# Attention and two MLPs on one core: the second MLP's first operands loaded during the last slots of the first MLP

## The chip, the core and the metric

The kernel runs on one core of one Trainium2 chip. The metric is the time of one execution on the device in microseconds (us), lower is better. Three runs of the kernel before took 1113.15, 1113.36 and 1116.99 us; their median is 1113.36 us.

## What is computed

A chunked attention, then two MLPs of 3072 tokens, one after the other, each 512 to 2048 to 512 wide:

```python
attn_out = _attn_ref(**attn_kwargs)             # 4 x 8 x 768 x 64, chunks of 32 with 8 memory keys
x = attn_out.transpose(0, 2, 1, 3).reshape(B * S, H * D)
h = x @ w_in                                    # first MLP
x = np.where(h > 0.0, h, np.exp(np.minimum(h, 0.0)) - 1.0) @ w_out
r = np.maximum(x @ w_in2, 0.0)                  # second MLP
out = (s * (r * r) + b) @ w_out2
```

Every large product is made of three products of halves: an operand is split into a rounded part (hi) and the rest (lo), and hi·hi, hi·lo and lo·hi are added up (`mm3`, lines 323 to 325).

## The kernel before

**First MLP.** The tokens are cut into eight tiles of 384. For each tile there are 16 slots, one for each 128 of the 2048 hidden columns. Slot `c` of tile `t` is `h1(t, c)`: twelve matmuls into a PSUM bank `psH`, the activation on ScalarE (ACT) and VectorE (DVE) (lines 347 to 349), and the split into `gh` and `gl`. Two slots later `out1(t, c)` adds the slot's part to four accumulators `acc` with twelve more matmuls. After a tile's last slot `put_out` copies the four accumulators into `big` tiles, two on ACT and two on DVE (lines 377 and 379), and SyncE (SP) stores them to `y_dram` (line 380). A `big` tile comes from the pool `op`, two buffers in tiles 5 to 7, or, where `big_tile` is told `spare`, from the pool `wst` of three. Attention runs beside the first tiles.

**Weights.** The first MLP's weights stay in SBUF, split, in the pool `wp`: 32 tiles of 4 KB a partition, two for each slot number (`w0_c` for `h1`, `w1_c` for `out1`). The second MLP's weights are turned into seven block combinations for each 256 hidden columns (`prepare`, tiles 5 to 7, pool `prep`) and stored to `s_dram`. `prepared` spreads 160 such steps over the half slots of tiles 5 to 7.

**Second MLP.** It works on three tiles of 1024 tokens with a seven-product scheme (`ORDER`). `load_blocks(t)` loads four blocks of 512 KB from `y_dram` (line 611), makes three differences on DVE (line 614), and splits seven operands `xc`: seven copies on ACT (line 618) and seven subtractions on DVE (line 181). `next_piece` loads the weight pieces `ws`, 256 KB each, twelve buffers deep (line 596). `first_layer` multiplies, and takes its first two products out of PSUM with `aside` (ACT, line 630) into the pool `evp`, since the third accumulates in the first one's bank.

**What sets the order.** Each engine and SP's queue run their instructions in the order in which a scheduler wrote them down, which follows the order of the program's calls and may move an instruction ahead. Between the MLPs all pools of the first are closed (`pctx.close(); mctx.close()`), then the pools of the second are opened on the same memory, and `for _ in load_blocks(0): pass` comes before the first matmul:

```python
    pctx.close()
    mctx.close()
...
    for _ in load_blocks(0):
        pass
    for t in range(NT2):
```

At the start SP loads `kb` and `q` of unit 0, the two scalars `s_sb` and `b_sb` (lines 461 and 462; 128 elements of 4 bytes each), and then `kb` and `q` of unit 1.

Of the kernel before, what the change touches and what calls it, by code (L numbers as in the profile page):

```python
# [8 lines left out]
F32 = mybir.dt.float32  # L9
I32 = mybir.dt.int32  # L10
# [18 lines left out]
NU0 = 6  # L29
HF = 6  # L30
TATT = 5
MICRO = 8
HN, NT2 = 512, 3
ORDER = (1, 2, 6, 5, 7, 3, 4)
# [18 lines left out]
def tile_attention_then_two_mlps(ctx, tc, q_in, k_in, v_in, w1, w2, s_in, b_in, out):  # L53
# [34 lines left out]
    const = ctx.enter_context(tc.tile_pool(name="const", bufs=1))  # L88
    dp = ctx.enter_context(tc.tile_pool(name="dp", bufs=1, space=bass.MemoryType.DRAM))
    mctx = ExitStack()  # L90
    wp = mctx.enter_context(tc.tile_pool(name="wp", bufs=1))
    wst = mctx.enter_context(tc.tile_pool(name="wst", bufs=3))
    one = mctx.enter_context(tc.tile_pool(name="one", bufs=1))
    xp = mctx.enter_context(tc.tile_pool(name="xp", bufs=1))
# [18 lines left out]
    def f(t):  # L113
        return t.bitcast(F32)
# [3 lines left out]

    def load_w(w, c, i):

        r = wp.tile([P, DM, 2], I32, tag=f"w{i}_{c}", name=f"raw{i}_{c}")
        nc.sync.dma_start(out=r, in_=w[c, i].bitcast(I32).rearrange("p (n z) -> p n z", z=2))
        return r

# [14 lines left out]
    def split_w(c, i, raw):  # L139

        t = wst.tile([P, DM], I32, tag="t", name="t")
        yield from to_f32(raw, t)
        nm = "io"[i]
        parts = wp.tile([P, 2, DM], F32R, tag=f"w{i}_{c}", name=f"w{i}_{c}")
        hi, lo = parts[:, 0], parts[:, 1]
        nc.scalar.activation(out=hi, in_=f(t), func=AF.Copy)
        sub(lo, f(t), hi)
        W[nm, c], WT[nm, c] = (hi, lo), parts
        yield
# [30 lines left out]
    def sub(lo, src, hi):  # L180
        return nc.vector.tensor_tensor(out=lo, in0=src, in1=f(hi), op=ALU.subtract)  # L181

    def big_tile(n, spare=False):

        if spare:
            return wst.tile([P, DM], F32, tag="t", name="big")[:, :n]
        return op[-1].tile([P, n], F32, tag="big", name="big")
# [173 lines left out]
    def put_out(t, c, n):  # L361

        split, t0 = t == 0, starts[t] * U
        if c == HF and split:
            for m in range(KT):
                PART[m] = big_tile(n)
                nc.sync.dma_start(out=PART[m], in_=part_dram[:, m, :n])
        if c == NF - 1 or c == HF - 1 and split:
            for m, acc in enumerate(ACC[t]):
                with tc.high_priority(400):  # L370
                    if c == NF - 1 and split:
                        o = PART.pop(m)
                        nc.vector.tensor_tensor(out=o, in0=o, in1=acc[:, :n], op=ALU.add)
                    else:
                        o = big_tile(n, m == 3 and t >= 2)
                        if m % 2:
                            nc.vector.tensor_copy(o, acc[:, :n])
                        else:
                            nc.scalar.activation(out=o, in_=acc[:, :n], func=AF.Copy)  # L379
                nc.sync.dma_start(out=y_dram[:, m, t0:t0 + n] if c == NF - 1 else part_dram[:, m, :n], in_=o)  # L380

    def out1(t, c):
        n = sizes[t] * U
# [43 lines left out]
    def prepare_all():  # L427
        for layer in range(2):
            for i in range(NF // 2):
                yield from prepare(layer, i)  # L430
# [27 lines left out]

    warm(6, pt.rearrange("p h n -> p (h n)")[:, :2 * U])
    set_up()  # L460
    nc.sync.dma_start(out=s_sb, in_=s_in.to_broadcast([P, 1]))
    nc.sync.dma_start(out=b_sb, in_=b_in.to_broadcast([P, 1]))

    nload = [1, 0]

# [27 lines left out]
    def weights_to(w, n, ahead):  # L493

        while wnext[0] < min(n, MICRO * NF):
            k, m = divmod(wnext[0], MICRO // 2)
            c, i = divmod(k, 2)
            load_ws(w, k + 1 + ahead)
            if m == 0:
                wsteps[:] = [split_w(c, i, wraw[k])]  # L500
            next(wsteps[0])
            wnext[0] += 1
# [7 lines left out]
    def beside(want, weights):  # L510
# [6 lines left out]
            weights_to(w, n0 + (n - n0) * (done[0] - d0) // (want - d0), ahead)  # L517
        weights_to(w, n, ahead)

    def mlp1_step(t, c):  # L520

        phase[0] = (1 if c < HF else 3) if t == 0 else 2 if t == 1 else 4

        a0, total, k, ks = done[0], 0, 0, 1
        if t == 0 and c < HF:
            a0, total, k, ks = ready[0], ready[1] - ready[0], c, HF
        elif t == 0:
            a0, total, k, ks = ready[1], ready[2] - ready[1], min(c - HF, NF - HF - 4), NF - HF - 3
        elif 1 < t < TATT:
            a0, total, k, ks = ready[2], len(steps) - ready[2], NF * (t - 2) + c, NF * (TATT - 2)  # L530

        wt = [(w1, 0, 4)] * 2
        if t == 0 and c < HF:
            n0, n1 = 12, 8 * HF + 12
            wt = [(w1, max(n0 + (n1 - n0) * (2 * c + z) // (2 * HF), MICRO * (c + z)), 4) for z in (1, 2)]
        elif t == 1:
            n0 = 8 * HF + 12
            wt = [(w1, max(n0 + (MICRO * NF - n0) * (2 * c + z) // 28, MICRO * (c + z)), 4) for z in (1, 2)]
        if c == 0 and t == TATT:
            actx.close()  # L540
            op.append(mctx.enter_context(tc.tile_pool(name="op2", bufs=2)))
            p2["prep"] = mctx.enter_context(tc.tile_pool(name="prep", bufs=2, reuse_waits="tile"))
            p2["steps"] = prepare_all()
        if t < 2:
            weights_to(w1, MICRO * (c + 1), 4)
        h1(t, c)
        beside(a0 + total * (2 * k + 1) // (2 * ks), wt[0])
        prepared(t, 2 * c + 1)
        yield
        beside(a0 + total * (2 * k + 2) // (2 * ks), wt[1])  # L550
        prepared(t, 2 * c + 2)
        if c == NF - 4 and 1 <= (t or 1) < NTILE1 - 1 and t != 1:
            load_x(max(t, 1) + 1)
        yield

    def prepared(t, n):

        want = NPREP * (2 * NF * (t - TATT) + n) // (2 * NF * (NTILE1 - TATT))
        while t >= TATT and p2["n"] < want:
            next(p2["steps"])  # L560
            p2["n"] += 1
# [11 lines left out]
    for slot in seq[-2:]:  # L573
# [2 lines left out]
    pctx.close()  # L576
    mctx.close()

    xcp, yrp, wsp, g2p, evp, ghp, outp = (
        ctx.enter_context(tc.tile_pool(name=nm, bufs=k, reuse_waits="tile"))  # L580
        for nm, k in (("xcp", 1), ("yrp", 4), ("wsp", 12), ("g2p", 4), ("evp", 5), ("ghp", 3), ("outp", 4)))
    psp = ctx.enter_context(tc.tile_pool(name="psp", bufs=8, space=PSUM, reuse_waits="tile"))

    def bank(nm):
        return psp.tile([P, HN], F32, tag="b", name=nm)

    pieces = [(0, i, j) for i in range(NF // 2) for j in ORDER] + [(1, i, j) for j in ORDER for i in range(NF // 2)]
    pieces = pieces * NT2
    ws, used = [], [0]

    def next_piece(layer, i, j):

        while len(ws) < min(used[0] + 11, len(pieces)):
            lay, ii, jj = pieces[len(ws)]
            w = wsp.tile([P, 2, 2 * P], F32R, tag="ws", name="ws")
            nc.sync.dma_start(out=f(w), in_=s_dram[lay, ii, :, PIECE[jj]])
            ws.append(w)
        assert pieces[used[0]] == (layer, i, j)
        used[0] += 1
        return ws[used[0] - 1]  # L600

    XC = {}

    def load_blocks(t):

        t0 = t * 2 * HN
        xc = XC[t] = {j: xcp.tile([P, 2, 2, HN], F32R, tag=f"xc{j}", name=f"xc{j}") for j in ORDER}
        b12 = yrp.tile([P, 2, HN], F32, tag="yr", name="b12")
        b11, b21, b22 = (f(xc[j][:, 1]) for j in (1, 2, 3))
        for o, r, z in ((b11, 0, 0), (b12, 0, 1), (b22, 1, 1), (b21, 1, 0)):  # L610
            nc.sync.dma_start(out=o, in_=y_dram[:, 2 * r:2 * r + 2, t0 + z * HN:t0 + (z + 1) * HN])
        t3, t2, t4 = (yrp.tile([P, 2, HN], F32, tag="yr", name=nm) for nm in ("t3", "t2", "t4"))
        for o, x, y in ((t3, b22, b12), (b12, b12, b11), (t2, b22, b12), (t4, b21, t2)):
            nc.vector.tensor_tensor(out=o, in0=x, in1=y, op=ALU.subtract)
            yield
        src = {1: b11, 2: b21, 6: t2, 5: b12, 7: t3, 3: b22, 4: t4}
        for j in ORDER:
            nc.scalar.activation(out=xc[j][:, 0], in_=src[j], func=AF.Copy)
            sub(xc[j][:, 1], src[j], xc[j][:, 0])
            yield  # L620

    def add(o, x, y):
        return nc.vector.tensor_tensor(out=o, in0=x, in1=y, op=ALU.add)
# [89 lines left out]
                        nc.scalar.activation(out=r, in_=o[m], func=AF.Copy)  # L713
                    put(r, t, 2 + m, 0)

    for _ in load_blocks(0):
        pass
    for t in range(NT2):
        gs = [g2p.tile([P, 4, 2, HN], F32, tag="g", name="g2") for _ in range(NF // 4)]
        for i in range(NF // 2):  # L720
# [59 lines left out]
```

## Time and profile before

| | |
|---|---|
| median of three runs | 1113.36 us |
| the profiled execution: its own time | 1114.08 us |
| the profiled execution: its span | 1112.3 us |
| mean granted TensorE clock | 0.985 |
| TensorE (PE) busy | 1072.5 us, 96% of the span |
| DVE busy | 785.8 us, 71% |
| ACT busy | 593.3 us, 53% |
| DMA: HBM read and written | 164.89 MB and 47.45 MB, 191 GB/s |

Busy times are shares of the whole span, and a matmul's end is modelled. Where PE waits is read from the slices of the span, and then from the timeline of the place. The execution that was profiled has a time of its own, 1.78 us over its span.

### The profile page before, as it was taken

What the parts mean: (1) busy time and instruction counts of PE and PEld (TensorE: products, weight loads), DVE (VectorE), ACT (ScalarE), POOL (GpSimd) and SP (SyncE); (2) the same over time, 40 slices, a digit from 0 to 9 for tenths busy, and PEclk for the clock granted to TensorE, in tenths of its full rate; (3) what the DMA queues carried; (4) which work ended last, traced back from release to release, by engine and by line L of the source; (5) the groups of instructions that cost most, each with busy time, mean ns of one, the idle gap of its engine ahead of it and who ended that gap; (6) DMA issues with size and microseconds to landing.
All of it is one profiled execution on the core that took longest, in us unless ns stands there. A gap on an engine that the chain in (4) does not pass through costs nothing.

```text
span 1112.3 us, 20640 instructions
## 1 busy us (share of the span) xinstructions
PE 1072.5 (96%) x8206; PEld 965.0 (87%) x8206; DVE 785.8 (71%) x1299; ACT 593.3 (53%) x939; POOL 0.7 (0%) x6
## 2 busy tenths in 40 slices
PE   6989999999999999999999599999999999999998
PEld 4879999999999999999999577778888788888886
DVE  6899856777777777998882267598356697266854
ACT  3888544344344337887773355555255654355442
POOL 0000000000000000000000000000000000000000
PEclk8899999999999999999999889999999999999999
DMA  8955032433434217889770476777866777776674
GB/s 307 372 199 223 1 107 86 150 133 100 140 115 143 88 40 251 332 312 325 286 281 30 162 222 187 229 221 211 252 190 191 226 215 211 225 197 190 190 213 128
DMA packets 98112, 213.70 MB, mean 192 GB/s; under 512 B 9952, under 2 KB 27360, under 8 KB 95968
## 3 DMA queue, kind: packets, MB, share of 16 engines
q1 hardware_dynamic: 98016, 212.38, 58.8%
q8 instruction: 65, 1.06, 0.4%
q14 instruction: 31, 0.25, 0.1%
HBM read 164.89 MB, written 47.45 MB: 191 GB/s over the span
## 4 chain that ended last, share of the span: by engine, by line
PE 75%; DVE 9%; DMA 7%; ACT 5%; issue 2%; SPq 0%; DVEq 0%; ACTq 0%
PE psH L323 13%; PE psH L324 12%; PE psH L325 12%; PE psL L324 6%; PE psL L325 6%; PE psL L323 6%; PE acc L323 5%; PE acc L325 5%; PE acc L324 5%; DMA xc<-y_dram 2%; DMA raw<-w 2%; PE psVS L275 1%; DVE pt L255 1%; DVE t L132 1%; ACT raw L129 1%
## 5 line engine op out<-in xcount | busy, mean ns | idle before, releaser
L323 PE MATMUL acc<-gh,w 128*128 128x384 f32 x512 | 171.6, 337 | 5.1 <-ACT big L379 2.3
L323 PE MATMUL psH<-xh,w 128*128 128x384 f32 x512 | 174.3, 341 | 0.9 <-DVE g L349 0.6
L324 PE MATMUL psH<-xl,w 128*128 128x384 f32 x512 | 172.6, 337 | 0.2 <-DVE xl L181 0.2
L325 PE MATMUL psH<-xh,w 128*128 128x384 f32 x512 | 172.4, 337 | 0.0
L324 PE MATMUL acc<-gl,w 128*128 128x384 f32 x512 | 171.5, 335 | 0.0
L325 PE MATMUL acc<-gh,w 128*128 128x384 f32 x512 | 171.3, 335 | 0.0
L323 PE MATMUL psH<-xc,ws 128*128 128x512 f32 x336 | 133.6, 402 | 13.4 <-DMA ws<-s_dram 11.8
L679 ACT ACTIVATE g2h<-g 128x1024 fp32r<-128x1024 f32 x84 | 88.9, 1059 | 90.1 <-PE psL L325 89.8
L324 PE MATMUL psL<-g2l,ws 128*128 128x512 f32 x336 | 130.9, 390 | 1.9 <-DVE g2l L181 1.9
L324 PE MATMUL psH<-xc,ws 128*128 128x512 f32 x336 | 131.8, 392 | 0.9 <-DVE xc L181 0.9
L325 PE MATMUL psH<-xc,ws 128*128 128x512 f32 x336 | 131.8, 392 | 0.0
L325 PE MATMUL psL<-g2h,ws 128*128 128x512 f32 x336 | 130.7, 389 | 0.0
L181 DVE TENSOR_TENSOR g2l<-g,g2h 128x1024 fp32r<-128x1024 f32 x84 | 102.2, 1223 | 39.5 <-ACT g2h L679 39.2
L323 PE MATMUL psL<-g2h,ws 128*128 128x512 f32 x336 | 130.1, 389 | 0.0
L347 ACT ACTIVATE g<-psH 128x384 f32<-128x384 f32 x128 | 62.6, 489 | 116.6 <-PE psH L325 77.0
L177 ACT ACTIVATE gh<-g 128x384 fp32r<-128x384 f32 x128 | 67.0, 523 | 87.9 <-DVE g L349 87.1
L349 DVE SCALAR_TENSOR_TENSOR g<-g,psH 128x384 f32<-128x384 f32 x128 | 70.6, 551 | 58.9 <-ACT g L348 57.8
L323 PEld LDWEIGHTS acc<-gh,w 128*128 128x128 f32 x512 | 95.9, 188 | 7.5 <-ACT big L379 2.9
L323 PEld LDWEIGHTS psH<-xh,w 128*128 128x128 f32 x512 | 96.9, 189 | 3.2 <-DVE g L349 1.2
L324 PEld LDWEIGHTS psH<-xl,w 128*128 128x128 f32 x512 | 96.9, 189 | 0.4 <-DVE xl L181 0.4
L325 PEld LDWEIGHTS psH<-xh,w 128*128 128x128 f32 x512 | 97.0, 189 | 0.0
L324 PEld LDWEIGHTS acc<-gl,w 128*128 128x128 f32 x512 | 96.1, 188 | 0.4 <-DVE gl L181 0.4
(97 smaller groups left out, 1668.2 us busy)
## 6 DMA issues: line engine op xcount, KB each, us to landing
ws<-s_dram SPq DMA_DIRECT2D x336, 256.0 KB, 3.0
raw<-w SPq DMA_DIRECT2D x64, 512.0 KB, 5.8
s_dram<-right SPq DMA_DIRECT2D x16, 1024.0 KB, 4.8
kb<-k SPq DMA_DIRECT2D x24, 512.0 KB, 5.6
v<-v SPq DMA_DIRECT2D x24, 512.0 KB, 4.7
s_dram<-left SPq DMA_DIRECT2D x16, 768.0 KB, 4.1
q<-q SPq DMA_DIRECT2D x24, 256.0 KB, 5.4
y_dram<-big SPq DMA_DIRECT2D x32, 192.0 KB, 2.0
```

The costliest lines, as they stand in the source:

```text
L129: nc.scalar.activation(out=low, in_=low.bitcast(U32), func=AF.Copy, scale=2.0 ** -29 * (1 - 2.0 ** -15), bias=-0.4999)
L132: nc.vector.scalar_tensor_tensor(out=t, in0=high, scalar=3, in1=low, op0=ALU.logical_shift_left, op1=ALU.bitwise_or)
L177: return nc.scalar.activation(out=hi, in_=src, func=AF.Copy)
L181: return nc.vector.tensor_tensor(out=lo, in0=src, in1=f(hi), op=ALU.subtract)
L255: nc.vector.transpose(out=pt[k * CH:(k + 1) * CH, :, rows], in_=sm[rows, :, z, n0:n0 + CH])
L275: nc.tensor.matmul(ps[r % 2 * D:(r % 2 + 1) * D, z, o:o + CH], v[rows, (r * NC + c) * D:(r * NC + c + 1) * D], pt[rows, r, cs], start=True ...
L323: nc.tensor.matmul(o, sa(a[0]), sb(b[0]), start=first, stop=False, skip_group_check=again)
L324: nc.tensor.matmul(o, sa(a[0]), sb(b[1]), start=False, stop=False, skip_group_check=again)
L325: return nc.tensor.matmul(o, sa(a[1]), sb(b[0]), start=False, stop=last, skip_group_check=again)
L347: nc.scalar.activation(out=g[:, :n], in_=ps[:, :n], func=AF.Relu, scale=-1.0)
L349: nc.vector.scalar_tensor_tensor(out=g[:, :n], in0=g[:, :n], scalar=-1.0, in1=ps[:, :n], op0=ALU.add, op1=ALU.max)
L679: nc.scalar.activation(out=gh, in_=g[:, block], func=AF.Copy)
```

## The change

- The pool `wp` is cut in two: `wpa` with the sixteen weight tiles of slots 0 to 7 (`NFREE = 8`), on the right side of the memory, and `wpb` with the others. `prep` moves to the right side, next to `wpa`.
- In tile 7, before `h1` of slot 10, `prep` and `wpa` are closed and the second MLP's pools `xcp`, `yrp` and `wsp` are opened there. `load_blocks(0)` now also loads the first twelve weight pieces, and is advanced three steps after each of slots 10 to 15.
- `prepared` has to be through with its 160 steps 16 half slots earlier.
- In tiles 5 to 7 three of the four `big` tiles come from `wst`. In tile 7 the stores are issued by ACT in place of SP.
- `s_sb` and `b_sb` are loaded at the start of tile 5, and no more at the start of the kernel.

```diff
-    wp = mctx.enter_context(tc.tile_pool(name="wp", bufs=1))
+    early = [ExitStack(), ExitStack()]
+    wps = [early[0].enter_context(tc.tile_pool(name="wpa", bufs=1, side="right")),
+           mctx.enter_context(tc.tile_pool(name="wpb", bufs=1))]
...
-                        o = big_tile(n, m == 3 and t >= 2)
+                        o = big_tile(n, t >= TATT and m > 0 or m == 3 and t >= 2)
...
-                nc.sync.dma_start(out=y_dram[:, m, t0:t0 + n] if c == NF - 1 else part_dram[:, m, :n], in_=o)
+                store = nc.scalar if t == NTILE1 - 1 else nc.sync
+                store.dma_start(out=y_dram[:, m, t0:t0 + n] if c == NF - 1 else part_dram[:, m, :n], in_=o)
...
     set_up()
-    nc.sync.dma_start(out=s_sb, in_=s_in.to_broadcast([P, 1]))
-    nc.sync.dma_start(out=b_sb, in_=b_in.to_broadcast([P, 1]))
...
+    def load_blocks(t):
...
+        for o, r, z in ((b11, 0, 0), (b12, 0, 1), (b22, 1, 1), (b21, 1, 0)):
+            nc.sync.dma_start(out=o, in_=y_dram[:, 2 * r:2 * r + 2, t0 + z * HN:t0 + (z + 1) * HN])
+        if t == 0:
+            load_pieces(12)
...
+    def open_second():
+
+        for nm, k in (("xcp", 1), ("yrp", 4), ("wsp", 12)):
+            p2[nm] = ctx.enter_context(tc.tile_pool(name=nm, bufs=k, side="right", reuse_waits="tile"))
+        p2["blocks"] = load_blocks(0)
...
+            p2["prep"] = early[1].enter_context(tc.tile_pool(name="prep", bufs=2, side="right", reuse_waits="tile"))
             p2["steps"] = prepare_all()
+            nc.sync.dma_start(out=s_sb, in_=s_in.to_broadcast([P, 1]))
+            nc.sync.dma_start(out=b_sb, in_=b_in.to_broadcast([P, 1]))
...
+        if t == NTILE1 - 1 and c == NFREE + 2:
+            early[1].close()
+            early[0].close()
+            open_second()
         h1(t, c)
...
+        if t == NTILE1 - 1 and c >= NFREE + 2:
+            for _ in range(3):
+                next(p2["blocks"], None)
...
-        want = NPREP * (2 * NF * (t - TATT) + n) // (2 * NF * (NTILE1 - TATT))
+        want = min(NPREP * (2 * NF * (t - TATT) + n) // (2 * NF * (NTILE1 - TATT) - 2 * (NF - NFREE)), NPREP)
...
-    for _ in load_blocks(0):
-        pass
+    assert next(p2["blocks"], None) is None
```

**SP's queue at the end of the first MLP.** `s_dram<-right` and `left` are the stores of prepared weights, `xc` and `b` the four blocks of the second MLP's first tile, `ws` its weight pieces, the last `b` a block of its second tile. Before:

```order
L424 DMA s_dram<-right 128x2048
L380 DMA y_dram<-big 128x384 x2
L611 DMA xc_7722<-y_dram 128x2x512
L380 DMA y_dram<-big 128x384 x2
L611 DMA b_7729<-y_dram 128x2x512
L611 DMA xc_7727<-y_dram 128x2x512
L611 DMA xc_7723<-y_dram 128x2x512
L596 DMA ws<-s_dram 128x512 x13
L611 DMA b_8662<-y_dram 128x2x512
```

Now:

```order
L428 DMA s_dram<-right 128x2048
L531 DMA ws<-s_dram 128x512 x12
L550 DMA xc_7501<-y_dram 128x2x512
L550 DMA b_7508<-y_dram 128x2x512
L550 DMA xc_7506<-y_dram 128x2x512
L550 DMA xc_7502<-y_dram 128x2x512
L550 DMA b_8666<-y_dram 128x2x512
L531 DMA ws<-s_dram 128x512 x49
```

The last tile's stores have left the queue, and the twelve pieces now stand ahead of the blocks.

**DVE in slots 10 to 13 of tile 7, now.** `g` and `gl` are the two DVE instructions of a slot; the first `gl` is slot 10's, the last `g` slot 13's.

```order
L184 TENSOR_TENSOR gl<-g,gh 128x384
L555 TENSOR_TENSOR t_7537<-xc_7506,b_7508 128x1024
L555 TENSOR_TENSOR b_7508<-b_7508,xc_7501 128x1024
L352 SCALAR_TENSOR_TENSOR g<-g,psH 128x384
L555 TENSOR_TENSOR t_7538<-xc_7506,b_7508 128x1024
L184 TENSOR_TENSOR gl<-g,gh 128x384
L555 TENSOR_TENSOR t_7539<-xc_7502,t_7538 128x1024
L184 TENSOR_TENSOR xc_7501<-xc_7501 128x1024
L184 TENSOR_TENSOR xc_7502<-xc_7502 128x1024
L352 SCALAR_TENSOR_TENSOR g<-g,psH 128x384
L184 TENSOR_TENSOR xc_7503<-t_7538,xc_7503 128x1024
L184 TENSOR_TENSOR gl<-g,gh 128x384
```

Before, all eleven instructions on `xc`, `t` and `b` stood behind the tile's last two `big` copies.

**ACT at the end of tile 5 and at the end of tile 7.** At the end of tile 5 before:

```order
L379 ACTIVATE big<-acc_5664 128x384
L177 ACTIVATE gh<-g 128x384
L422 ACTIVATE right<-sums 128x4x256
L379 ACTIVATE big<-acc_5666 128x384
L347 ACTIVATE g<-psH 128x384
```

Now:

```order
L382 ACTIVATE big<-acc_5677 128x384
L382 ACTIVATE big<-acc_5679 128x384
L180 ACTIVATE gh<-g 128x384
L426 ACTIVATE right<-sums 128x4x256
L350 ACTIVATE g<-psH 128x384
```

The second eviction has moved ahead of `gh` and `right`. At the end of tile 6 four instructions stood between the two evictions, and now one does. At the end of tile 7, now:

```order
L382 ACTIVATE big<-acc_7142 128x384
L384 DMA y_dram<-big 128x384
L382 ACTIVATE big<-acc_7144 128x384
L384 DMA y_dram<-big 128x384
L384 DMA y_dram<-big 128x384
L384 DMA y_dram<-big 128x384
L653 ACTIVATE m_7794<-psH 128x512
L653 ACTIVATE u_7812<-psH 128x512
```

ACT issues the four stores between its evictions and the second MLP's first `aside`, `m_7794`. The memory of `m_7794` is that of the `big` tile of `acc_7144`, so it waits for that tile's store.

## Rows read from the trace of the kernel before

**Rows 1.** The page, part 2: tenths of 40 slices, 27.8 us each.

```profile
PE   6989999999999999999999599999999999999998
...
PEclk8899999999999999999999889999999999999999
```

**Rows 2.** Windows: busy us of each engine (instructions), granted clock, DMA share, GB/s.

```profile
620.00:625.00 5.00, 5.00 (x30) 5.00 (x30) 1.11 (x2) 1.67 (x4) 0.00 (x0) 1.00 0.00 0
...
630.00:635.00 5.00, 0.00 (x0) 0.00 (x0) 0.00 (x0) 1.06 (x1) 0.00 (x0) 0.50 0.99 325
...
640.00:650.00 10.00, 8.96 (x29) 6.65 (x29) 9.46 (x9) 4.12 (x6) 0.00 (x0) 0.71 0.74 245
650.00:680.00 30.00, 30.00 (x131) 24.03 (x131) 16.54 (x17) 15.80 (x20) 0.00 (x0) 1.00 0.69 200
```

**Rows 3.** Chain that ended last, between the MLPs: start, us, what.

```profile
625.39 1.85 DMA y_dram<-big
...
629.28 6.78 DMA xc<-y_dram
```

**Rows 4.** Timeline, PE, between the MLPs: start, us, instruction [idle before <- releaser].

```profile
626.06 0.34 PE L325 MATMUL acc<-gh,w 128*128 128x384 f32 x1
638.19 0.76 PE L323 MATMUL psH<-xc,ws 128*128 128x512 f32 x1 [11.79 <-DMA ws<-s_dram]
...
647.09 0.39 PE L324 MATMUL psH<-xc,ws 128*128 128x512 f32 x1
...
649.36 0.39 PE L323 MATMUL psH<-xc,ws 128*128 128x512 f32 x1
```

**Rows 5.** Instructions on the tile xc: count, ns min/median/max, first and last start.

```profile
L618 ACT ACTIVATE xc<-xc x9: 1041/1059/1065, 630.6 to 881.4; 128x1024 fp32r<-128x1024 f32 x9
...
L614 DVE TENSOR_TENSOR t<-xc,b x6: 1218/1223/1226, 636.2 to 908.8; 128x1024 f32<-128x1024 f32 x6
```

**Rows 6.** Timeline, DVE, slots 11 and 15 of tile 7.

```profile
604.63 0.55 DVE L349 SCALAR_TENSOR_TENSOR g<-g,psH 128x384 f32<-128x384 f32 x1 [2.46 <-ACT g L348]
605.78 0.56 DVE L181 TENSOR_TENSOR gl<-g,gh 128x384 fp32r<-128x384 f32 x1 [0.59 <-ACT gh L177]
...
621.27 0.55 DVE L349 SCALAR_TENSOR_TENSOR g<-g,psH 128x384 f32<-128x384 f32 x1 [2.46 <-ACT g L348]
```

**Rows 7.** Chain that ended last: first matmul of out1 in slot 11 of tile 7.

```profile
611.83 0.17 PE acc L323
```

**Rows 8.** Windows, tile 7 after the last prepared weights are stored.

```profile
586.00:594.00 8.00, 8.00 (x49) 8.00 (x48) 2.22 (x4) 3.09 (x6) 0.00 (x0) 1.00 0.01 3
```

**Rows 9.** DMA issues on s_dram: count, ns, first and last start.

```profile
L424 SPq DMA_DIRECT2D s_dram<-right x16: 319/326/446, 437.9 to 582.6; - x16
```

**Rows 10.** Waits of PE at the ends of tiles 5 and 6: us, times, longest.

```profile
PE acc L323 <- ACT big L379: 1.0, 1, 1.0
...
PE acc L323 <- ACT big L379: 1.3, 1, 1.3
```

**Rows 11.** Timeline, ACT: the second eviction of tiles 5 and 6.

```profile
498.17 0.47 ACT L379 ACTIVATE big<-acc 128x384 f32<-128x384 f32 x1
...
566.31 0.48 ACT L379 ACTIVATE big<-acc 128x384 f32<-128x384 f32 x1
```

**Rows 12.** Timeline, SP and DVE, the start of the kernel.

```profile
1.65 0.58 SPq L461 DMA_DIRECT2D s_sb<-s  x1
...
2.90 0.59 SPq L165 DMA_DIRECT2D kb<-k  x1
...
12.22 0.69 DVE L228 TENSOR_REDUCE nmx<-psS 128x8 f32<-128x512 f32 x1 [2.11 <-PE psS L216]
```

**Rows 13.** DMA, 0 to 20 us: GB/s in 40 slices of 0.5 us.

```profile
GB/s 0 0 0 82 254 393 311 356 160 17 25 17 17 41 189 344 348 422 414 426 422 410 434 401 430 401 410 414 397 414 426 377 410 393 389 365 356 381 320 221
```

**Rows 14.** Instructions on the tile big: DMA from issue to landing.

```profile
DMA to landing us min/median/max: 1.9/2.0/5.8
```

**Rows 15.** Timeline, SP: the first weight pieces.

```profile
630.43 14.52 SPq L596 DMA_DIRECT2D ws<-s_dram  x13
```

More of the change, by code (lines that the diff above doesn't have):

```diff
@@ L31 @@
 TATT = 5
+NFREE = 8
 MICRO = 8
@@ L119, in load_w @@
     def load_w(w, c, i):
-        r = wp.tile([P, DM, 2], I32, tag=f"w{i}_{c}", name=f"raw{i}_{c}")
+        r = wps[c >= NFREE].tile([P, DM, 2], I32, tag=f"w{i}_{c}", name=f"raw{i}_{c}")
         nc.sync.dma_start(out=r, in_=w[c, i].bitcast(I32).rearrange("p (n z) -> p n z", z=2))
@@ L143, in split_w @@
         nm = "io"[i]
-        parts = wp.tile([P, 2, DM], F32R, tag=f"w{i}_{c}", name=f"w{i}_{c}")
+        parts = wps[c >= NFREE].tile([P, 2, DM], F32R, tag=f"w{i}_{c}", name=f"w{i}_{c}")
         hi, lo = parts[:, 0], parts[:, 1]
@@ L518, in beside, with load_pieces, next_piece @@
         weights_to(w, n, ahead)
+    pieces = [(0, i, j) for i in range(NF // 2) for j in ORDER] + [(1, i, j) for j in ORDER for i in range(NF // 2)]
+    pieces = pieces * NT2
+    ws, used = [], [0]
+    def load_pieces(n):
+        while len(ws) < min(n, len(pieces)):
+            lay, ii, jj = pieces[len(ws)]
+            w = p2["wsp"].tile([P, 2, 2 * P], F32R, tag="ws", name="ws")
+            nc.sync.dma_start(out=f(w), in_=s_dram[lay, ii, :, PIECE[jj]])
+            ws.append(w)
+    def next_piece(layer, i, j):
+        load_pieces(used[0] + 11)
+        assert pieces[used[0]] == (layer, i, j)
+        used[0] += 1
+        return ws[used[0] - 1]
+    XC = {}
+    def load_blocks(t):
+        t0 = t * 2 * HN
+        xc = XC[t] = {j: p2["xcp"].tile([P, 2, 2, HN], F32R, tag=f"xc{j}", name=f"xc{j}") for j in ORDER}
+        b12 = p2["yrp"].tile([P, 2, HN], F32, tag="yr", name="b12")
+        b11, b21, b22 = (f(xc[j][:, 1]) for j in (1, 2, 3))
+        for o, r, z in ((b11, 0, 0), (b12, 0, 1), (b22, 1, 1), (b21, 1, 0)):
+            nc.sync.dma_start(out=o, in_=y_dram[:, 2 * r:2 * r + 2, t0 + z * HN:t0 + (z + 1) * HN])
+        if t == 0:
+            load_pieces(12)
+        t3, t2, t4 = (p2["yrp"].tile([P, 2, HN], F32, tag="yr", name=nm) for nm in ("t3", "t2", "t4"))
+        for o, x, y in ((t3, b22, b12), (b12, b12, b11), (t2, b22, b12), (t4, b21, t2)):
+            nc.vector.tensor_tensor(out=o, in0=x, in1=y, op=ALU.subtract)
+            yield
+        src = {1: b11, 2: b21, 6: t2, 5: b12, 7: t3, 3: b22, 4: t4}
+        for j in ORDER:
+            nc.scalar.activation(out=xc[j][:, 0], in_=src[j], func=AF.Copy)
+            sub(xc[j][:, 1], src[j], xc[j][:, 0])
+            yield
+    def open_second():
+        for nm, k in (("xcp", 1), ("yrp", 4), ("wsp", 12)):
+            p2[nm] = ctx.enter_context(tc.tile_pool(name=nm, bufs=k, side="right", reuse_waits="tile"))
+        p2["blocks"] = load_blocks(0)
     def mlp1_step(t, c):
@@ L541, in mlp1_step @@
             op.append(mctx.enter_context(tc.tile_pool(name="op2", bufs=2)))
-            p2["prep"] = mctx.enter_context(tc.tile_pool(name="prep", bufs=2, reuse_waits="tile"))
+            p2["prep"] = early[1].enter_context(tc.tile_pool(name="prep", bufs=2, side="right", reuse_waits="tile"))
             p2["steps"] = prepare_all()
+            nc.sync.dma_start(out=s_sb, in_=s_in.to_broadcast([P, 1]))
+            nc.sync.dma_start(out=b_sb, in_=b_in.to_broadcast([P, 1]))
         if t < 2:
             weights_to(w1, MICRO * (c + 1), 4)
+        if t == NTILE1 - 1 and c == NFREE + 2:
+            early[1].close()
+            early[0].close()
+            open_second()
         h1(t, c)
@@ L577, in tile_attention_then_two_mlps @@
     mctx.close()
-    xcp, yrp, wsp, g2p, evp, ghp, outp = (
+    g2p, evp, ghp, outp = (
         ctx.enter_context(tc.tile_pool(name=nm, bufs=k, reuse_waits="tile"))
-        for nm, k in (("xcp", 1), ("yrp", 4), ("wsp", 12), ("g2p", 4), ("evp", 5), ("ghp", 3), ("outp", 4)))
+        for nm, k in (("g2p", 4), ("evp", 5), ("ghp", 3), ("outp", 4)))
     psp = ctx.enter_context(tc.tile_pool(name="psp", bufs=8, space=PSUM, reuse_waits="tile"))
@@ L585, in bank @@
         return psp.tile([P, HN], F32, tag="b", name=nm)
[L587 to L620, printed above, removed]
     def add(o, x, y):
```

## The prediction

> **What bounds the kernel now.** I read the slices of the span first. PE is at nine tenths or more in nearly all of them, and one slice in the middle stands out, the 23rd, with a half, and with a clock below full in it and the next [rows 1]. That is the seam of the two MLPs. The windows around it show PE at work without a break until 625, idle from 630 to 635, where the granted clock is 0.50 (1.2 GHz), and busy again from 640 to 650, at a clock of 0.71; from 650 on it is full [rows 2]. The chain says why: the last tile's store has to leave its buffer (1.85 us), and then the second MLP's blocks take 6.78 us to land [rows 3]; only then come the differences, the splits and, behind the blocks in SP's queue, the weight pieces. PE waits 11.8 us for one of these [rows 4]. So PE sets the time, and what counts is what PE loses.
>
> **The seam: -17.0 us.** The last matmul of the first MLP begins at 626.06, and such a matmul follows the one before by 0.17 us [rows 4, 7]. From the second MLP's first matmul at 638.19 to the one at 649.36 there are 27 steps, all recorded, so the latter is its 28th. From the 18th, at 647.09, ten steps take 2.27 us, 0.227 each [rows 4]. Without a break the 28th would begin at 626.06 + 0.17 + 27 x 0.227 = 632.4. It begins at 649.36, 17.0 us later, and afterwards PE is full [rows 2], so the whole 17.0 us reaches the end. They are the wait of 11.8, and 5.2 us of short waits and of matmuls at the lower clock after the idle stretch [rows 2]. With operands and pieces there in time PE does not stop, and the clock has no reason to fall.
>
> **What has to be hidden, priced at nothing.** *DVE and ACT:* eleven DVE instructions of 1.22 us and seven ACT copies of 1.06 us [rows 5] move into slots 10 to 13, 13.4 and 7.4 us. A slot is 4.16 us (four of them between 604.63 and 621.27), and DVE has 1.1 us of its own in each [rows 6]: 13.4 + 4 x 1.1 = 17.8 us in 16.6, so DVE runs about 1.2 us into slot 14, plus at most two long instructions ahead of a slot's `g`, 2.4 us. The cover is that `out1` comes two slots later: slot 11's `g` begins at 604.63, its `gl` ends at 606.34, and PE wants it at 611.83 [rows 6, 7], 5.5 us of room against 3.6. ACT has room anyway. *The loads:* DVE's first difference has its turn after slot 10's `gl`, at 602.2. With 2.4 us for two long instructions and 1.7 for `g` to `gl`, blocks that land after 611.8 - 4.1 = 607.7 cost PE a microsecond each. The twelve pieces come first in SP's queue, behind the last stores of `prepare`. These are issued at 582.6 today [rows 9], and the new order has them about a slot earlier. Thirteen pieces took 14.5 us to issue when they shared the DMA with four blocks [rows 15]; now the DMA is free, a share of 0.01 [rows 8]. Even by that number, and with 6.8 us for the blocks [rows 3], the landing is 582.6 + 14.5 + 6.8 = 603.9, in time. *The earlier end of `prepare`:* the scheduler already runs it ahead, its last store being 24 us into tile 7 and not at its end [rows 9], so a limit 16 half slots earlier changes its pace little. *`s_sb` and `b_sb` in tile 5:* 1.2 us of SP's queue, ahead of raw weights that have that much room. If these covers were gone, the price is that of the third rival.
>
> **Ends of tiles 5 and 6: -2.0 us.** PE waits there 1.0 and 1.3 us for the second eviction on ACT [rows 10, 11]: at the end of tile 5 it stands behind `gh` and `right`. In the new order the two evictions are neighbours at the end of tile 5 and one `g` apart at the end of tile 6. The gain is at most 2.3. A raw conversion that waits for its load now stands ahead of the pair at the end of tile 6, so at worst PE loses there once more what it loses today, -1.3. I take 2.0, near the good end, since two and three instructions leave from between the evictions and PE's waits are no longer than these.
>
> **Start: -1.5 us.** `kb` of unit 1 is issued at 2.90 in place of 1.65, 1.25 us later for the two scalars [rows 12]. Worse, the DMA moves 311 to 393 GB/s until 4.0 us, and then 17 to 41 from 4.5 to 7.0, before the next load flows [rows 13]: about 2.5 us in which the 256 packets of 4 bytes stand ahead of it. DVE waits 2.11 us for that load's scores [rows 12]. The gain lies between 1.25, the issue alone, and 2.5, if the first steps follow; after 40 us other limits could eat it, and the scheduler also put the first steps of ACT and DVE in another order, so below I allow -2.1, that wait once more. I take 1.5. The Trainium skill, "DMA: Bandwidth & Descriptors", section "Why small descriptors are slow (HBM only)", charges a small packet a few cycles and 32 bytes. By it 256 packets on 16 engines cost next to nothing, and the sum would have 1.25 us here; the slices of 17 to 41 GB/s speak against it.
>
> **The first `aside`: +0.5 us.** Moving the stores to ACT adds four issues between the evictions and `m`, and `m` lies on the memory of a `big` tile whose store must land. The third accumulator is complete at 625.7, evicted by 626.2 (0.48 us [rows 11]); with two issues at some 0.33 each, which is what SP's take [rows 9], and 2.0 us to land [rows 14], `m` begins at 628.9 and, at half the columns of the 1.06 us copy [rows 5], ends at 629.4 or a little later. The 16th matmul needs it, and is due at 626.2 + 15 x 0.227 = 629.6. There is nearly no room; an issue from ACT is in no row. Between 0 and 3.8 us (a landing of 5.8, the longest [rows 14]) I take 0.5, near the median landing. The same page of the Trainium skill, section "Anatomy of one DMA — SWDGE (gpsimd) path", gives 2.0 us plus the bytes over 436 GB/s, an estimate of 2.45 us for these 192 KB. By it `m` would end 0.45 us later than by the row, and the sum stay as it is.
>
> **Sum.** 17.0 + 2.0 + 1.5 - 0.5 = 20.0 us off the profiled execution's own 1114.08 (its span of 1112.3 and 1.78 around it) is 1094.1. That execution lies 0.7 us above the median of the runs shown; I give **1094 us**.
>
> **Rivals.**
> *The seam closes, the rest does not come (13%).* The store that `m` waits for lands late (-3.8 us at most), and start and tile ends give nothing. For it: the room before the 16th matmul is a tenth of a microsecond. Against: the DMA is idle then but for these four stores. 17.0 - 3.8 = 13 us off: 1101.
> *The change does not do what it says (3%).* The operands' work would stay behind the last eviction, as the scheduler could have put it. Against: in the order now the first difference stands between slots 10 and 11. Time: 1113.
> *The blocks land late, and DVE stops in the middle of the first MLP (4%).* DVE works in order, so a difference that waits for its block holds back slot 11's `g`, and PE with it. From a landing at 607.7 on, PE loses all of the delay; with 20.5 us won elsewhere it is slower than before from 628 on. At 636.2, when DVE gets the blocks today (629.28 + 6.78 [rows 3]), PE would lose 28.5 us: net 8 slower, 1122. For it: the blocks stand behind twelve pieces, and these behind the last prepared weights. Against: after these stores the DMA has next to nothing to do until 625 [rows 2, 8], and their landing leaves 25 us up to 607.7 [rows 9].
>
> **How the numbers follow.** The forecast has 80%. Its own terms span from 17.0 + 2.3 + 2.5 = 21.8 off, 1092.3, to 17.0 - 1.3 - 2.1 - 3.8 = 9.8 off, 1104, where not all bad ends meet. The range 1090 to 1101 takes in the good end with 2 us for what I did not see, and the first rival, and leaves out the others. About 0.5%, 5.6 us, is what a measurement of this kernel can tell from no change. Forecast and first rival are faster by more: 93%; the second is the same: 3%; the third is slower: 4%.
>
> **What would show it.** Right: no PE idle above 1 us between the last `acc` and the first `psH<-xc` matmul, a granted clock of 1.00 throughout, the 28th matmul some 6 us after the last `acc` one; the first difference on DVE about slot 10 without a wait for its blocks; no wait of PE for `big` of tiles 5 and 6; the DMA at over 300 GB/s from 4 to 7 us and DVE's 2.11 us gone. Wrong: PE waiting for `g` or `gl` in slots 11 to 15, or for `m` at the 16th matmul by more than 1 us, or new waits in tiles 5 and 6 behind `prepare`.

## The result, and the profile after

The changed kernel takes 1097.18 us (median of 4 runs, 1095.98 to 1099.69) against 1113.26 for the kernel before beside it: a ratio of 0.9854, 95% interval 0.9824 to 0.9885. Measured a second time, among the experiments, it stood at 0.9884 (0.9865 to 0.9903). The profiled execution took 1097.48, its span 1095.7. The forecast was 1094 and its range 1090 to 1101: faster by over 0.5%, as forecast, and 3 us short of the gain.

Slices of the page after, against [rows 1]: PE has no weak slice in the middle any more, and the clock no dip.

```profile
PE   7999999999999999999999999999999999999998
...
PEclk7999999999999999999999999999999999999999
```

Windows at the seam after, against [rows 2]: PE is busy without a break, at a granted clock of 1.00, where it had stood at 0.50 and 0.71; DVE does the operands' work from 600 to 620 beside it.

```profile
600.00:610.00 10.00, 10.00 (x59) 10.00 (x58) 9.06 (x11) 7.78 (x12) 0.00 (x0) 1.00 0.07 7
610.00:620.00 10.00, 10.00 (x60) 10.00 (x59) 6.36 (x9) 3.86 (x8) 0.00 (x0) 1.00 0.12 45
620.00:630.00 10.00, 10.00 (x47) 8.35 (x46) 2.70 (x5) 2.53 (x5) 0.00 (x0) 1.00 0.64 192
630.00:640.00 10.00, 10.00 (x45) 8.27 (x45) 4.49 (x6) 4.90 (x6) 0.00 (x0) 1.00 0.71 200
```

Timeline of PE after, against [rows 4]: the first matmul of tile 5's first `out1`, the last `acc` matmul, the first and the 28th of the second MLP, which follows the last `acc` by 6.35 us where it took 23.30, and two of the second layer, 24 steps apart.

```profile
427.33 0.34 PE L326 MATMUL acc<-gh,w 128*128 128x384 f32 x1
...
620.95 0.34 PE L328 MATMUL acc<-gh,w 128*128 128x384 f32 x1
621.12 0.39 PE L326 MATMUL psH<-xc,ws 128*128 128x512 f32 x1
...
627.30 0.39 PE L328 MATMUL psH<-xc,ws 128*128 128x512 f32 x1
...
1059.61 0.40 PE L326 MATMUL psL<-g2h,ws 128*128 128x512 f32 x1
...
1065.21 0.40 PE L326 MATMUL psL<-g2h,ws 128*128 128x512 f32 x1
```

The same view of the kernel before, at the two places that were not shown: tile 5's first `out1`, and again 24 steps of the second layer.

```profile
429.92 0.33 PE L323 MATMUL acc<-gh,w 128*128 128x384 f32 x1
...
1059.71 0.39 PE L325 MATMUL psL<-g2h,ws 128*128 128x512 f32 x1
...
1065.15 0.39 PE L325 MATMUL psL<-g2h,ws 128*128 128x512 f32 x1
```

With these the span splits into four pieces that add up to all of it:

| piece | before | after | difference | forecast |
|---|---|---|---|---|
| start of the span to tile 5's first `out1` | 429.92 | 427.33 | -2.59 | -1.5 |
| from there to the last `acc` matmul | 196.14 | 193.62 | -2.52 | -2.0 |
| from there to the 28th matmul of the second MLP | 23.30 | 6.35 | -16.95 | -17.0 + 0.5 |
| from there to the end | 462.94 | 468.40 | **+5.46** | 0 |
| span | 1112.30 | 1095.70 | -16.60 | -20.0 |

The first three pieces gave 22.1 us, more than forecast. The last one gave 5.5 back, in a stretch where the program did not change: PE has the same instructions there, and a granted clock of 1.00. What changed is the pace of the second layer's 1008 matmuls. In the rows above 24 steps take 5.44 us before and 5.60 after: 0.227 and 0.233 us each. Over the last 336 of them, from the first start to the last, it is 75.93 and 78.17 us, 6.7 ns a matmul. 1008 x 6.7 ns is 6.7 us. The same stretches of all three tiles together grew by 6.2 us (230.33 to 236.49); the first layer's matmuls, at an unchanged 227 ns in the median, gave a little back. The tile's instructions (ns min/median/max), after:

```profile
L327 PE MATMUL psL<-g2l,ws x336: 394/396/502, 699.5 to 1091.3; 128*128 128x512 f32 x168
```

and before:

```profile
L324 PE MATMUL psL<-g2l,ws x336: 389/389/500, 721.5 to 1107.8; 128*128 128x512 f32 x168
```

No wait of PE grew there: its waits from 650 us on are 2.8 us before and 1.9 after. What did change is where the operands lie. The byte addresses in the two programs, per partition, and what is left when they are divided by 64:

| | pieces `ws` (stationary) | `xc` (moving, first layer) | `g2h`, `g2l` (moving, second layer) |
|---|---|---|---|
| before | 91328, rest 0 | 17600, rest 0 | 191680, rest 0 |
| after | 131040, rest 32 | 172000, rest 32 | 93376, rest 0 |

So there were two theories. T1: the two operands of a matmul stand differently within 64 bytes, and that costs. T2: it is the place, pieces high in memory and moving operands low.

### The profile page after: what moved, and what is told of

Its sections match the earlier page's. It is cut to its first block, busy times and chain, and to the rows that moved or that the text cites. A ratio compares the mean times of both kernels' runs of the same rounds, so it can differ in the third digit from the quotient of the medians.

```text
span 1095.7 us, 20629 instructions
## 1 busy us (share of the span) xinstructions
PE 1076.3 (98%) x8206; PEld 964.4 (88%) x8206; DVE 783.9 (72%) x1299; ACT 591.9 (54%) x939; POOL 0.7 (0%) x6
## 4 chain that ended last, share of the span: by engine, by line
PE 87%; DVE 6%; DMA 4%; ACT 3%; issue 1%; SPq 0%; ACTq 0%; DVEq 0%
PE psH L326 14%; PE psH L328 14%; PE psH L327 14%; PE psL L327 7%; PE psL L328 7%; PE acc L326 7%; PE psL L326 7%; PE acc L327 7%; PE acc L328 7%; DVE pt L258 2%; DMA xc<-y_dram 1%; PE psVS L278 1%; DMA xl<-x_dram 1%; PE psVS L219 1%; PE psV L278 1%
## 5 line engine op out<-in xcount | busy, mean ns | idle before, releaser
L328 PE MATMUL psL<-g2h,ws 128*128 128x512 f32 x336 | 132.9, 395 | 0.0
L326 PE MATMUL psL<-g2h,ws 128*128 128x512 f32 x336 | 132.5, 396 | 0.1
```

The lines of the kernel that those rows point to most:

```text
L326: nc.tensor.matmul(o, sa(a[0]), sb(b[0]), start=first, stop=False, skip_group_check=again)
L328: return nc.tensor.matmul(o, sa(a[1]), sb(b[0]), start=False, stop=last, skip_group_check=again)
```

## Experiments

Ratios are to the kernel before, measured beside each. "Stretch" is the time from the first to the last start of the last 336 matmuls of a layer.

**1. The pieces back at multiples of 64.**

```diff
     mctx = ExitStack()
+    rpad = ctx.enter_context(tc.tile_pool(name="rpad", bufs=1, side="right"))
+    rp = rpad.tile([P, 8], F32, name="rp")
...
+        nc.gpsimd.memset(rp, 0.0)
```

> The changed kernel with a pool of 32 bytes per partition put first on the right-hand side of memory, so that wpa, xcp and above all wsp (the stationary pieces of the second MLP) start at multiples of 64 bytes per partition instead of 32 past one (wsp at 131008 instead of 131040); the order of the work is that of the changed kernel. Theory T1 (the stationary piece and the moving operand of a second-layer matmul stand differently within 64 bytes, and this costs each of the 1008 matmuls some 6.4 ns): the second-layer matmuls go back from a mean of 233.3 ns start to start to 227, and the run takes 1097.2 - 6.4 = about 1091. Theory T2 (it is the place in memory, pieces above 128 KB and the moving operand below, whatever the offset): pace stays at 231 to 235 and the time at about 1097.

Measured: 1092.25 us, ratio 0.9786 (0.9769 to 0.9804). The profile's tile view of the padded kernel:

```profile
L330 PE MATMUL psL<-g2l,ws x336: 387/389/504, 700.6 to 1086.9; 128*128 128x512 f32 x168
```

The matmul is back at 389 ns and the stretch at 75.93 us. T1 holds, T2 falls: everything on the right side of the memory moved by 32 bytes, the pieces among it, and the pieces still lie high and the moving operands low. By spans the gain is 4.4 (1095.7 to 1091.3); by the runs it is more, 0.8% against the mean of the two measurements of the changed kernel. This version is faster than both kernels.

**2. The same difference made in the kernel before.**

```diff
-        for nm, k in (("xcp", 1), ("yrp", 4), ("wsp", 12), ...
+        for nm, k in (("xcp", 1), ("yrp", 4), ("lpad", 1), ("wsp", 12), ...
+    lp = lpad.tile([P, 8], F32, name="lp")
```

> The kernel before with 32 bytes per partition put in ahead of wsp, so that the pieces, and the pools g2p, evp and ghp after them, start 32 bytes past a multiple of 64, while xc and the first MLP's pools stay where they were. T1 (what counts is that stationary and moving operand stand differently within 64 bytes): the 1008 first-layer matmuls of the second MLP (piece shifted, xc not) become slow, 231 to 235 ns instead of 227, the second-layer ones (both shifted) stay at 227, and the run takes 1113.3 + 6.4 = about 1119.7. T1b (what counts is that a stationary piece starts off a multiple of 64): both kinds slow, 1113.3 + 12.8 = about 1126. T2 (place in memory): nothing changes, 1113.

Measured: 1117.79, ratio 1.0021 (1.001 to 1.0032). Tile views, a first-layer row of the kernel before, and then a first-layer and a second-layer row of the edited kernel:

```profile
L324 PE MATMUL psH<-xc,ws x336: 387/389/792, 642.1 to 1031.6; 128*128 128x512 f32 x168
...
L324 PE MATMUL psH<-xc,ws x336: 389/395/793, 643.5 to 1035.6; 128*128 128x512 f32 x168
...
L324 PE MATMUL psL<-g2l,ws x336: 387/389/504, 724.8 to 1111.8; 128*128 128x512 f32 x168
```

The slow kind is the first layer, whose operands now differ; the second layer, with both operands 32 past, is fast. So a rest of 32 is not slow in itself, the difference is: T1, not T1b. The price was 2.4 us and not 6.4: before, the first layer's stretch takes 77.16 us and not 75.93, because single steps of 231 to 236 ns lie in it anyway; with the shift it takes 78.36. Three times 1.2 is 3.6.

**3. The mirror: the moving operand shifted.** The pad stands ahead of `ghp` in place of `wsp`.

```diff
+        for nm, k in (..., ("evp", 5), ("lpad", 1), ("ghp", 3),
```

> The mirror of e2_before_pieces_32: the kernel before with 32 bytes per partition put in ahead of ghp alone, so that the moving operand of the second-layer matmuls starts 32 bytes past a multiple of 64 while the stationary pieces and xc stay at multiples of 64. If any difference between the two operands within 64 bytes costs 6 to 8 ns a matmul, the second-layer ones take 231 to 235 ns start to start and the first-layer ones 227: before + 6.4 us at most, a ratio to before of about 1.003 to 1.006. Rival: only a stationary piece off a multiple of 64 under a moving operand on one is slow: nothing changes, ratio 1.000.

Measured: 1120.81, ratio 1.0059 (1.0039 to 1.0079), 6.6 us; the second layer's stretch is 78.17 us.

```profile
L324 PE MATMUL psL<-g2l,ws x336: 392/394/503, 721.5 to 1112.6; 128*128 128x512 f32 x168
```

The difference costs from either side.

**4. How fine must the match be?** On experiment 1's kernel, the moving operands 16 bytes past.

```diff
-                gh, gl = (ghp.tile([P, 2, HN], F32R, tag=nm, name=nm) for nm in ("g2h", "g2l"))
+                gh, gl = (ghp.tile([P, 2 * HN + 16], F32R, ...)[:, 4:2 * HN + 4].rearrange("p (i n) -> p i n", i=2)
+                          for nm in ("g2h", "g2l"))
```

> The kernel of e1_right_pad with the moving operands g2h and g2l of the second-layer matmuls 16 bytes per partition past a multiple of 64 (tiles of 1040 columns, used from column 4 on), the stationary pieces at multiples of 64. It asks how fine the match of the two operands has to be. If any difference within 64 bytes costs: the second-layer matmuls take 231 to 235 ns start to start, e1 + 6 us, about 1098. If only the 32-byte half counts: 227 ns, about 1092.

Measured, one run: 1096.98. The stretch is 77.60 us, 5.0 ns a matmul above the matched one, with single steps from 225 to 240. So a difference of 16 bytes costs most of it too, and it is not only the 32-byte half that counts. The edit also makes the two tiles longer, 4160 bytes in place of 4096, which was not tried by itself.

**5. The scalars first again.**

```diff
+    nc.sync.dma_start(out=s_sb, in_=s_in.to_broadcast([P, 1]))
+    nc.sync.dma_start(out=b_sb, in_=b_in.to_broadcast([P, 1]))
...
-            nc.sync.dma_start(out=s_sb, in_=s_in.to_broadcast([P, 1]))
-            nc.sync.dma_start(out=b_sb, in_=b_in.to_broadcast([P, 1]))
```

> The changed kernel with the two loads of the scale and the bias put back at the kernel's start, all else as changed. If the start's term of the prediction is right, 1.5 us are lost: 1097.2 + 1.5 = about 1098.7; by the reading of the two traces (the last matmul of the first MLP begins 5.1 us earlier, 2.3 of it from the ends of tiles 5 and 6) it is up to 2.8: about 1100. The DMA rate should show its dip again at 4.5 to 7 us and the wait for q at its old length. Rival: the start is bound by something else, and the time stays within 0.5 of 1097.2.

Measured: 1100.75, ratio 0.9869 (0.9851 to 0.9886), which the two measurements of the changed kernel enclose, so the runs don't settle it. The traces show more. DMA, 0 to 20 us in slices of 0.5 us, with the scalars first:

```profile
GB/s 0 0 0 115 139 401 356 401 140 46 33 9 17 82 262 393 385 414 447 410 426 410 418 442 381 418 426 401 414 377 401 410 401 410 389 426 401 324 258 201
```

and after, where DVE's wait for unit 1's scores is 0.53 us (`nmx` at 9.81) in place of 1.79 in experiment 5 (at 11.25) and 2.11 before:

```profile
GB/s 0 0 0 57 205 426 356 377 397 336 303 209 381 410 418 410 426 418 418 426 385 381 217 348 447 393 369 361 401 418 393 426 414 397 172 49 25 33 0 66
```

The hole of 9 to 46 GB/s is the two loads' work. Tile 5's first `out1` begins at 430.14 with it, 1.2 to 2.8 us later than in the two traces of the changed kernel (428.96 and 427.33). In the four profiled executions with the scalars first (before and experiments 2, 3 and 5) it lies at 429.92 to 430.98, in the nine with them in tile 5 at 425.45 to 428.96, in the mean 2.6 us earlier. These kernels differ in other ways too, so the sign is clear and the size is not.

**6. The old rule for output buffers.**

```diff
-                        o = big_tile(n, t >= TATT and m > 0 or m == 3 and t >= 2)
+                        o = big_tile(n, m == 3 and t >= 2)
```

> The changed kernel with the old rule for the outputs of the tiles (the first MLP's outputs of tiles 5 and 6 do not alternate with the second kind of buffer; PE's order is untouched). The prediction's term of 2.0 (bounds -1.3 to +2.3): the two PE waits of 1.0 and 1.3 at the ends of tiles 5 and 6 come back, the last matmul of the first MLP begins 2.3 later, and the run takes 1097.2 + 2.3 = about 1099.5. Rival: the waits went because of the earlier work of the other engines, not because of the buffers: no wait comes back, 1097.2.

Measured: 1102.43, ratio 0.9886 (0.9868 to 0.9903). The changed kernel stood at 0.9854 and at 0.9884, so the runs don't settle this one either. The trace does. Waits of PE from 480 to 626, of which the changed kernel has none:

```profile
PE acc L326 <- ACT big L382: 3.0, 2, 1.6
```

The stretch from tile 5's first `out1` to the last `acc` matmul is 197.14 us, 3.5 more than after. The buffers took the waits away, as the prediction had it.

**7. The operands' work written after the first MLP.** On experiment 1's kernel, two ways: all of it late, and only the differences and splits late. The edit of the first:

```diff
-        if t == NTILE1 - 1 and c >= NFREE + 2:
-            for _ in range(3):
-                next(p2["blocks"], None)
...
-    assert next(p2["blocks"], None) is None
+    for _ in p2["blocks"]:
+        pass
```

> The kernel of e1_right_pad (the changed kernel with its pieces back at multiples of 64 bytes) with the second MLP's loads, differences and splits taken out of the slots and issued after the first MLP, as in the kernel before; pools, stores on ACT, buffers and start stay as changed. If the seam's term of the prediction (17.0) is right, the 28th matmul of the second MLP begins again some 23 us after the last acc matmul and the run takes e1's 1092.3 + 17.0 = about 1109. Rival: the new place of the pools or the stores on ACT closed part of the seam by themselves (the loads no longer wait for the pools of the first MLP to close): then 3 to 6 us of the 17 do not come back, 1103 to 1106.

> The kernel of e1_right_pad with the loads of blocks and pieces left in slot 10, but the differences and splits taken out of the slots and issued after the first MLP. It parts the 17.0 of the seam into the transfers and the vector work. By the trace of before, the first matmul needs the split of one block behind the last evictions (0.5 us each), up to four differences of 1.22, a copy of 1.06 and a subtraction of 1.22: PE would stand still for some 3 to 7 us, and then each operand's subtraction of 1.22 keeps up with the 1.36 that six matmuls take. Theory: the greater part of the 17.0 is the transfers' (store, blocks, pieces) and the clock lost behind the long idle stretch; 1092.3 + 4 to 9 = 1096 to 1101. Rival: the vector work is what counts, the transfers were hidden behind it: 1092.3 + 12 or more, over 1104.

Measured: 1091.58, ratio 0.9794 (0.9773 to 0.9814), and 1090.03, ratio 0.978 (0.9759 to 0.9801). Every expectation missed: nothing came back. The timelines of the first of the two kernels, SP and then DVE, say why:

```profile
578.64 7.96 SPq L534 DMA_DIRECT2D ws<-s_dram  x12
587.01 0.38 SPq L553 DMA_DIRECT2D xc<-y_dram  x1
```

```profile
598.29 1.22 DVE L558 TENSOR_TENSOR t<-xc,b 128x1024 f32<-128x1024 f32 x1
...
615.21 1.22 DVE L186 TENSOR_TENSOR xc<-t,xc 128x1024 fp32r<-128x1024 f32 x1
```

The scheduler puts the loads and splits into the same slots, wherever the code calls them. With the pools opened at slot 10, the place of the calls in the code is worth nothing.

**8. The old addresses.** On the kernel of experiment 7 (all late), the three pools opened on the left after the first MLP.

```diff
-        if t == NTILE1 - 1 and c == NFREE + 2:
-            early[1].close()
-            early[0].close()
-            open_second()
...
-            p2[nm] = ctx.enter_context(tc.tile_pool(name=nm, bufs=k, side="right", reuse_waits="tile"))
+            p2[nm] = ctx.enter_context(tc.tile_pool(name=nm, bufs=k, reuse_waits="tile"))
...
     mctx.close()
+    early[1].close()
+    early[0].close()
+    open_second()
```

> The kernel of e5_all_late (loads and splits written after the first MLP, which cost nothing there, because the scheduler still moved them into slots 9 to 14) with one thing changed: the pools xcp, yrp and wsp are opened after the first MLP on the left-hand side, at the addresses that they have in the kernel before, on the memory of the weight slots that are used until the end. Theory M (the memory alone sets the seam, not the place in the code): the 28th matmul of the second MLP begins again some 23 us after the last acc matmul in place of 6.2, and the run takes 1091.5 + 17 = about 1108. Rival S (the stores on ACT, or the earlier end of prepare, closed the seam): it stays closed, 1091.5.

Measured: 1102.32, ratio 0.9904 (0.9883 to 0.9925), 1.1% or 12 us above experiment 7. PE at the seam:

```profile
619.91 0.34 PE L331 MATMUL acc<-gh,w 128*128 128x384 f32 x1
626.45 1.51 PE L329 MATMUL psH<-xc,ws 128*128 128x512 f32 x2 [6.20 <-DMA ws<-s_dram]
630.00 0.77 PE L329 MATMUL psH<-xc,ws 128*128 128x512 f32 x1 [2.03 <-DMA ws<-s_dram]
...
638.56 0.39 PE L331 MATMUL psH<-xc,ws 128*128 128x512 f32 x1
```

The 28th matmul comes 18.65 us after the last `acc` matmul, against 6.40 in experiment 7 and 23.30 before. So the pools at the old addresses bring 12.3 us back: PE's waits, and steps of 0.43 us behind them, at a granted clock of 0.74 to 0.75 (the mean of a part at 1.2 GHz and one at 2.4). That is not the wait of the kernel before, though. SP's waits from 590 to 640, in the kernel before and then here:

```profile
SPq L380 <- ACT big L379: 43.4, 2, 42.4
...
SPq L553 <- PE acc L331: 39.3, 2, 20.3
SPq L534 <- DMA y_dram<-big: 6.0, 1, 6.0
```

In experiment 8 the blocks wait for PE's last use of the memory, and the first piece behind them for the landing of one of the last tile's stores. In the kernel before, SP stands 42.4 us at the first of that tile's stores, until the eviction that fills its buffer, and the first block, which stands behind two stores, is issued at 626.39 without a wait of its own. The addresses are the old ones, but not what lies there: before, the three pools take the place of the weights of slots 0 to 11; in experiment 8 it is the weights of slots 8 to 15, output buffers and the first MLP's inputs. So experiment 8 shows that memory still in use brings most of the seam back. It does not show that memory kept the loads late in the kernel before; there the trace shows the stores ahead of them. Taking only the stores off SP's queue in the kernel before was not tried.

The other 4.7 us are gone even here. In the kernel before, ACT's last eviction waits for the store of the buffer that it takes, and that eviction's store and the last blocks' loads follow on SP:

```profile
627.35 0.49 ACT L379 ACTIVATE big<-acc 128x384 f32<-128x384 f32 x1 [1.98 <-DMA y_dram<-big]
```

In experiment 8 the same eviction waits 0.55, for PE, and SP has issued all four block loads by 617.5, ahead of the stores. Which of buffers and queue counts more was not tried.

**9. The stores back on SP.** On experiment 1's kernel.

```diff
-                store = nc.scalar if t == NTILE1 - 1 else nc.sync
-                store.dma_start(...)
+                nc.sync.dma_start(...)
```

> The kernel of e1_right_pad with the last tile's stores back on SP's queue in place of ACT's. The prediction charged the stores on ACT with 0.5 us (0 to 3.8), the trace shows less than 0.1. Theory: with the loads already landed, SP is free at the end of the first MLP, ACT saves four issues, and m still waits for the landing of one store: no change, 1092 within 2 us, and the 28th matmul of the second MLP begins 6.2 to 6.4 us after the last acc matmul. Rival: on SP the stores stand behind weight pieces that wait for their buffers; m waits for them and PE with it: 2 us or more are lost at the 16th matmul.

Measured: 1089.7, ratio 0.9785 (0.9761 to 0.981); the 28th matmul 6.40 us after the last `acc`. `m` on ACT:

```profile
623.50 0.60 ACT L655 ACTIVATE m<-psH 128x512 f32<-128x512 f32 x1 [2.13 <-DMA y_dram<-big]
```

With the operands there early, it does not matter which queue stores.

**10. The changed kernel once more.**

> The changed kernel as it is, beside the others on the same chip, so that the runs of a few microseconds' difference have a reference of their own: ratio to before 0.985 as measured first (interval 0.982 to 0.989); the second-layer matmuls again at 231 to 235 ns; the first matmul of the second MLP within 0.2 us of the last acc matmul. Against it e1_right_pad should stand at 0.993 to 0.995, e3_scalars_first at 1.0015 to 1.0025 and e4_old_buffers at 1.002 to 1.004.

Measured: 1100.92, ratio 0.9884. The second layer's steps are again 231 to 235 ns, the stretch 78.17 us; the 28th matmul comes 6.35 us after the last `acc`. The ratio lies at the upper end of the first measurement's interval, so differences of 0.2% between runs of separate occasions decide nothing here.

## Why the prediction came out as it did

*The seam: right, to 0.1 us.* PE runs through, the clock stays at 1.00, the first difference begins on DVE at 597.20 right behind slot 10's `gl`, without a wait for its block. No wait for `g` or `gl` reached PE. The blocks had been issued by 588.9, so the rival of a late landing, which began at 607.7, never came near; nor did the earlier end of `prepare` or the scalars in tile 5 show a wait of PE. The work did move into slots 10 to 13, as forecast: DVE's last subtraction begins at 612.92, ahead of slot 14's `g`. Which part of the change moved it is shown in part. Once the new pools are there, the place of the calls does nothing (experiment 7), nor does the queue of the stores (experiment 9), and pools on memory in use lose 12.3 of the 17.0 again (experiment 8). Whether another queue for the stores would have been enough in the kernel before is open.

*The first `aside`: too dear by 0.5.* ACT's timeline after:

```profile
620.80 0.49 ACT L382 ACTIVATE big<-acc 128x384 f32<-128x384 f32 x1 [0.55 <-PE acc L328]
620.87 1.37 ACTq L384 DMA_DIRECT2D y_dram<-big  x3
623.39 0.60 ACT L653 ACTIVATE m<-psH 128x512 f32<-128x512 f32 x1 [2.10 <-DMA y_dram<-big]
```

`m` ends at 623.99; the 16th matmul is due at 621.12 + 15 x 0.227 = 624.5. The prediction put two issues of 0.33 between the third eviction and its landing of 2.0. The eviction ends at 621.29 and `m` begins 2.10 later, so the issues ahead cost 0.1 beside a landing of 2.0, the 2.45 that the prediction set beside that row did not show, and half a microsecond of room was left.

*Ends of tiles 5 and 6: 2.5 in place of 2.0.* The two waits of 2.3 are gone [rows 10], and the stretch gained 2.5. Experiment 6 brings back 3.0 of waits and 3.5 in all.

*Start: 2.6 in place of 1.5, by the two profiled executions.* That is near the upper bound, by which all of the DMA's hole counts and not only the issue; experiment 5 by itself leaves 1.2 to 2.8. The rule of the Trainium skill, "DMA: Bandwidth & Descriptors", section "Why small descriptors are slow (HBM only)", by which the prediction would have had 1.25 here, does not explain the hole: in the slices of experiment 5 the two scalars' packets hold the queue at 9 to 46 GB/s for 2 us. The time alone does not speak against it.

*The step that failed* is one that the prediction did not have: that moving pools is free for the work that uses them later. It priced the work that was moved and looked for waits, and took the second MLP's pace of 0.227 [rows 4] as given. The new places put pieces and second-layer operands 32 bytes apart within 64, and 1008 matmuls at 6.7 ns took back 5.5 to 6.7 us. Without that term the sum of the measured gains is 22.1, and the profiled execution's 1114.08 would have become 1092.0; the four kernels with matched operands and a closed seam took 1089.7 to 1092.25.

## What to carry to other kernels

Where a scheduler orders the work, the line that calls a load may decide nothing (experiment 7): ask the trace what the load waits for. Here it was memory still in use in experiment 8, and a store ahead of it in its queue in the kernel before. When pools move, compare the addresses of each matmul's two operands: with 512 columns of four bytes, rests by 64 that differ by 16 or 32 bytes cost 5 to 7 ns of 227, up to 3%, in no wait that a profile lists. The sign in a trace is a slower step from one matmul's start to the next (227 to 233 ns) at the same clock and shape. The median duration moved with it here (389 to 396 ns), but in the first MLP it also moved where the step did not.

## What was not expected of the hardware

The price of the operands' relative address is the finding: 0 against 32 and 32 against 0 bytes cost 6.7 ns a matmul in the second layer, 0 against 16 cost 5.0, 32 against 32 nothing. The Trainium skill, "SBUF — State Buffer", section "Operand start alignment", asks only that an operand start at a multiple of its element size, and says of its runs that they timed nothing; the runs here time it. Why it costs is open: no run shows the mechanism. Open too is why the first MLP hardly suffers: eight of its weight slots lay 32 past a multiple of 64 under moving operands at rest 0, with matmuls of 336 ns in place of 334 in the median, but the way from tile 5's first `out1` to the last `acc` matmul took 193.62 us so and 193.27 with the pad, 0.35 for three tiles. These have 384 columns and a pace of 0.173 us. And there the loss is not where the operands differ: in the kernel after, the blocks of twelve matmuls on slots 0 to 7 keep their 173.4 ns a step, and those that take 175.4 have matched operands and come right behind such a block (`h1` of slots 8 to 10, and `out1` of slots 14 and 15 between the next tile's first slots). So that a difference of the rests costs is shown for the second MLP's matmuls of 512 columns, and not as a rule for every matmul.
